# Four-layer kernel: explicit per-engine sequences in place of priorities, two weight pieces moved from the ACT queue to the sync queue, bulk weights on the sync queue

## The chip, the cores and the metric

The kernel runs on one core of one Trainium2 chip. The metric is device microseconds (us) of one execution, the median of several runs. The engines are PE (matrix multiply; PEld is its weight load), DVE (vector), ACT (scalar, with the exponential and the logarithm), POOL (GpSimd) and SP (sync, which here only issues DMAs). Each engine executes its own instruction stream strictly in order and waits on semaphores; a DMA queue of an engine is fed by instructions of that same stream, so an issue that waits holds everything behind it on that engine.

## What is computed

Four layers follow each other on one tensor x of 2048 tokens by 448 features, all in bf16: attention (A), gated MLP (B), attention, gated MLP, each on a layer-normalized x and added back to x. Layers 0 and 2 share the attention weights, layers 1 and 3 the MLP weights.

```python
def _A_ref(x, wqkv, wo):                    # 16 heads of 28, window of 8 tokens, step 2
    qkv = (x @ wqkv).reshape(B, S, 3, H, Dh) ...
    idx = pos[:, None] - (jnp.arange(8) * 2)[None, :]
    logits = jnp.einsum("bhsd,bhswd->bhsw", q, k[idx]) * Dh ** -0.5
    attn = softmax(where(idx >= 0, logits, -1e9))
    return einsum("bhsw,bhswd->bhsd", attn, v[idx]) ... @ wo
def _B_ref(x, w_gate, w_up, w_down):        # F = 1792
    return ((x @ w_gate) * (x @ w_up)) @ w_down

x = x + _A_ref(_layernorm(x), wqkv, wo); x = x + _B_ref(_layernorm(x), w_gate, w_up, w_down)
x = x + _A_ref(_layernorm(x), wqkv, wo); x = x + _B_ref(_layernorm(x), w_gate, w_up, w_down)
```

## The kernel before

**Tiling.** Tokens are cut into chunks of 256 or 512 per layer (`ACH`, `BCH`); a chunk of layer l is called A0j, B1j, A2j or B3j, and `SEQ` gives the order in which chunks are planned (A00 A01 B10 A02 B11 ...), so that layers overlap. A matmul uses 64 of the 128 rows of the array, and two of them run side by side on the two halves; "a pair" below means such two. The main tiles are these.

- Layer norm (`ln_chunk`, L772 to L809): DVE takes statistics (`bn`, `mv`), ACT a logarithm and an exponential (`lnv`, `rstd`), DVE writes `xn_sb`. For layer 0 PE transposes it (L803, "Tps" below) and DVE or ACT copies the result to `xnTa` (L809, "T"). Later layers transpose by DMA on SP (L796).
- Query and key (`qk_chunk`): PE multiplies `xnTa` by `WQK`; one of ACT and DVE copies the bank pair to `qk` (L895, "QK(layer, chunk, part)"). Four rows of some parts are written to a DRAM tensor `vt` by small DMAs on SP (L904) and read back transposed (L915), as a part of the values.
- Value (`v_group`, L987), scores (`attn_front`: PE L1007, "S"; ACT exponential L1014; DVE mask L1024), attention times value (`attn_back`: PE L1044, "AV"; copies L1055; normalization L1069 to L1082), output projection (`y_blocks`, "Y", x updated at L1099).
- MLP (`b_chunk`): a unit is 14 matmuls of `xnTb` by `WGU` (gate and up on the two halves), then ACT copies the gate (L1135), DVE multiplies by up into `hT` (L1138), and PE multiplies `hT` by `WD` ("D").

L534 is the helper `pair` from which nearly all large matmuls are issued. L537 is its strip form: a score or AV burst of 64 small matmuls can be woven with large matmuls cut into four strips of 32 columns each (`WEAVE`).

**PSUM.** Eight banks; most users take a pair, and a bank is free again when its last reader has run.

**The order of the work.** `Sched` holds every operation with its dependencies and an estimated time. `schedule` runs the estimates as a simulation while the program is built; in before, whenever an engine is free it picks the ready operation of the lowest priority number (`prio` plus the tables `PR`, `XP`, `JP`, `HEAD_P`, `ATT_P`), with limits on banks (`A_CAP`, `B_CAP`). What comes out is a fixed order for each engine, and `emit` writes it with semaphore waits. At run time there is no choice: the program is the order.

**The head.** x and the weights come by DMA in pieces: x block 0 ("x0"), block 1 ("x0b"), blocks 2 and 3 ("x0h"), then blocks 4 to 7, 8 to 11 and 12 to 15 ("x1", "x2", "x3"). The query/key weights come in four pieces into a staging area in `hT` (`load_stage`, "stg0" to "stg3"), and eight copies (L709, "wqk(piece, half)") on ACT, DVE and POOL spread them into `WQK`; L717 ("wqp") adds the rows for `vt` later and has to wait until the query/key matmuls of chunk A01 are done, since they read the same tile. PE meanwhile runs 25 filler pairs on zeros (`WARM + FILL`, L700). POOL also builds masks (`MT`, `MK`) and a tile of ones (`ones32`, key `c_ones`), which a DMA on SP writes to `vt` ("vones", L624).

**The bulk weights** are `wo_g` (output projection), `WGU` (gate and up, two halves each: wg0, wu0, wg1, wu1) and `WD` (wd0 to wd3). In before they wait for x block 8; wg goes on SP and wu on ACT at once, `wo_g` waits for wu1 to land, wd0 for `wo_g`, and each next wd for the one before.

## Time and profile before

| | us |
|---|---|
| median of 3 runs | 391.18 |
| all three | 390.90, 391.18, 392.06 |
| the profiled execution | 392.05 |
| its span, first to last instruction | 390.3 |

The granted PE clock is 1.000 over the whole span. The table by stretches of the span (us; PE, DVE and ACT are busy times) shows where PE is not busy:

| stretch | PE | DVE | ACT | DMA GB/s |
|---|---|---|---|---|
| 0 to 9 | 7.74 | 5.17 | 4.85 | 248 |
| 9 to 16 | 6.47 | 6.95 | 4.34 | 287 |
| 16 to 46 | 28.07 | 23.14 | 26.76 | 156 |
| 46 to 75 | 26.39 | 24.47 | 19.32 | 53 |
| 75 to 390 | 312.85 | 216.18 | 145.52 | 38 |

In the last row PE is busy for 99.3% of the time. What is not busy before 75 us is 1.26 + 0.53 + 1.93 + 2.61 = 6.33 us. In views by line, a row names line, engine, operation, output<-input and count, then busy time and mean nanoseconds, then the idle time of the engine in front and what ended it.

### The profile page before, as it was taken

To read this page: it belongs to the slowest core of one execution; us is meant where nothing else is said; L and a number is where in the kernel's file an instruction comes from. 1 tells how busy PE (TensorE), PEld (TensorE's weight loads), DVE (VectorE), ACT (ScalarE), POOL (GpSimd) and SP (SyncE) were. 2 spreads that over 40 slices of the span, in tenths; PEclk is the share of its full clock that TensorE was granted. 3 is DMA by queue.
4 is the path that set the end of the run, shared out by engine and by line. 5 is a ranking of instruction groups with operands and counts; after the bars stand their busy time and mean duration, and the time that the engine had idled before them with its cause. 6 is when DMAs were issued, how large, how long until landed. Compare 5 with 4: busy or idle time off the path is not lost.

```text
span 390.3 us, 14405 instructions
## 1 busy us (share of the span) xinstructions
PE 381.5 (98%) x6394; PEld 213.8 (55%) x6394; DVE 275.9 (71%) x606; ACT 200.8 (51%) x386; POOL 8.3 (2%) x38
## 2 busy tenths in 40 slices
PE   8999989999999999999999999999999999999997
PEld 3555468554555544544456678545445544544584
DVE  6976789899649798496459965287676875467452
ACT  4797886664506676053544645055642542344150
POOL 7010000000000000000000000000000000000000
PEclk9999999999999999999999999999999999999999
DMA  7973532404302413221150204403230212100201
GB/s 258 263 210 92 131 41 56 58 11 83 41 2 53 61 21 50 49 29 29 22 55 15 41 13 33 82 26 52 37 64 29 40 34 50 50 2 2 51 23 47
DMA packets 54753, 22.50 MB, mean 58 GB/s; under 512 B 44884, under 2 KB 54692, under 8 KB 54692
## 3 DMA queue, kind: packets, MB, share of 16 engines
q1 hardware_dynamic: 53188, 19.24, 25.8%
q10 hardware_dynamic: 1504, 2.35, 2.2%
q8 instruction: 50, 0.82, 0.9%
q14 instruction: 11, 0.09, 0.1%
HBM read 8.54 MB, written 2.71 MB: 29 GB/s over the span
## 4 chain that ended last, share of the span: by engine, by line
PE 93%; ACT 4%; DVE 2%; issue 1%; ACTq 0%; DVEq 0%
PE ps L534 83%; PE ps L1007 3%; PE ps L1044 2%; PE ps L700 2%; PE ps L537 2%; PE ps L1150 1%; ACT qk L895 1%; ACT xnTa L809 1%; ACT E_sb L1014 1%; ACT R_sb L1070 0%; ACT g_sb L1135 0%; DVE oT L1082 0%; ACT O_sb L1055 0%; DVE v_sb L987 0%; DVE R_sb L1069 0%
## 5 line engine op out<-in xcount | busy, mean ns | idle before, releaser
L534 PE MATMUL ps<-xnTb,WGU 64*128 64x512 bf16 (+1 forms) x1942 | 176.8, 333 | 0.8 <-issue 0.8
L534 PEld LDWEIGHTS ps<-xnTb,WGU 64*128 64x128 bf16 x1942 | 94.2, 94 | 72.1 <-issue 1.5
L1135 ACT ACTIVATE g_sb<-ps 128x512 bf16<-128x512 f32 (+1 forms) x140 | 71.1, 511 | 92.9 <-PE ps L534 87.7
L1138 DVE TENSOR_TENSOR hT<-g_sb,ps 128x512 bf16<-128x512 bf16 (+1 forms) x140 | 79.6, 575 | 35.9 <-ACT g_sb L1135 34.0
L534 PE MATMUL ps<-WD,hT 64*128 64x448 bf16 x824 | 81.8, 349 | 0.0
L1099 DVE TENSOR_TENSOR x_sb<-x_sb,ps 128x448 bf16<-128x448 bf16 x62 | 35.9, 616 | 40.9 <-PE ps L534 40.8
L534 PEld LDWEIGHTS ps<-WD,hT 64*128 64x128 bf16 x824 | 39.6, 94 | 36.0
L534 PE MATMUL ps<-xnTa,WQK 64*128 64x512 bf16 (+1 forms) x488 | 51.6, 352 | 0.3 <-ACT xnTa L809 0.2
L1014 ACT ACTIVATE E_sb<-ps 128x1024 bf16<-128x1024 f32 (+1 forms) x36 | 33.7, 981 | 20.9 <-PE ps L1007 20.6
L772 DVE BATCH_NORM_STATS2 st<-x_sb 128x6 f32<-128x448 bf16 x64 | 37.4, 610 | 1.6 <-DMA x_sb<-in_A_x_dram 1.6
L793 DVE TENSOR_SCALAR xn_sb<-x_sb,mv,rstd 128x512 bf16<-128x512 bf16 (+1 forms) x64 | 34.1, 570 | 0.9 <-ACT rstd L777 0.8
L534 PEld LDWEIGHTS ps<-xnTa,WQK 64*128 64x128 bf16 x488 | 22.9, 94 | 20.5 <-ACT xnTa L809 1.1
L895 ACT ACTIVATE qk<-ps 128x1024 bf16<-128x1024 f32 (+1 forms) x30 | 26.9, 923 | 10.5 <-PE ps L534 10.3
L534 PE MATMUL ps<-wo_g,oT 64*128 64x448 bf16 x252 | 29.3, 349 | 0.1
L1024 DVE TENSOR_TENSOR E_sb<-E_sb,MK 128x1024 bf16<-128x1024 bf16 (+2 forms) x40 | 23.7, 608 | 7.2 <-ACT E_sb L1014 7.0
L1082 DVE TENSOR_TENSOR oT<-O_sb,R_sb 128x480 bf16<-128x480 f32 (+3 forms) x36 | 21.6, 627 | 5.2 <-ACT R_sb L1071 4.7
L1055 ACT ACTIVATE O_sb<-ps 128x512 f32<-128x512 f32 (+3 forms) x22 | 11.5, 547 | 26.4 <-PE ps L1044 26.3
L1070 ACT ACTIVATE R_sb<-R_sb 128x480 f32<-128x480 f32 (+1 forms) x34 | 20.0, 601 | 8.6 <-DVE R_sb L1069 8.5
L1069 DVE STREAM_SHUFFLE R_sb<-O_sb 128x480 f32<-128x480 f32 (+1 forms) x34 | 22.3, 696 | 0.0
L534 PE MATMUL ps<-WV,xnTa 64*128 64x336 bf16 (+3 forms) x244 | 21.1, 304 | 0.2
L1071 ACT ACTIVATE R_sb<-R_sb 128x480 f32<-128x480 f32 (+1 forms) x34 | 19.6, 601 | 0.4
L534 PEld LDWEIGHTS ps<-wo_g,oT 64*128 64x128 bf16 x252 | 12.5, 94 | 11.8 <-DVE oT L1082 1.1
(59 smaller groups left out, 190.7 us busy)
## 6 DMA issues: line engine op xcount, KB each, us to landing
out_dram<-x_sb SPq DMA_DIRECT2D x15, 112.0 KB, 1.7
WGU<-in_B_w_up_dram ACTq DMA_DIRECT2D x2, 784.0 KB, 11.5
WGU<-in_B_w_gate_dram SPq DMA_DIRECT2D x2, 784.0 KB, 13.5
x_sb<-in_A_x_dram SPq DMA_DIRECT2D x3, 448.0 KB, 7.1
WD<-in_B_w_down_dram SPq DMA_DIRECT2D x2, 448.0 KB, 3.8
hT<-in_A_wqkv_dram ACTq DMA_DIRECT2D x3, 224.0 KB, 3.5
WD<-in_B_w_down_dram SPq DMA_DIRECT2D x2, 336.0 KB, 3.9
vt<-qk SPq DMA_DIRECT2D x42, 16.0 KB
```

The lines of the kernel that those rows point to most:

```text
L534: return lambda E: E.matmul(out(), lhs(), rhs(), start=start, stop=stop)
L772: sc.add("dve", one(lambda E, B=B: E.bn_stats(st6[:, B, :], x_sb[:, B, :]), ("bn", li, B)), 525.0, deps=[("x", li - 1, B)] + ([("xn", li - ...
L793: sc.add("dve", one(lambda E, B=B, dst=dst, src=src: E.tensor_scalar(dst, src, mv[:, B, 0:1], rstd[:, B:B + 1], ALU.subtract, ALU.mult), ( ...
L895: return E.activation(dst, src, ACT.Copy) if hasattr(E, "activation") else E.tensor_copy(dst, src)
L1014: return E.activation(E_sb[:, slot, 2 * hp:2 * hp + 2, 0:w], ps[:, b0:b0 + 2, 0:w], ACT.Exp, scale=SCALE)
L1024: return E.tensor_tensor(e, e, m, ALU.mult)
L1069: sc.add("dve", one(lambda E: E.stream_shuffle(R_sb[:, rs, 0:w], O_sb[:, os_, 0:w], [DH] * 32), ("Rs", li, qb)), dve_est(w) + 100.0, deps= ...
L1070: sc.add("act", one(lambda E: E.activation(R_sb[:, rs, 0:w], R_sb[:, rs, 0:w], ACT.Ln), ("Rl", li, qb)), act_est(w, False), deps=[("Rs", l ...
L1082: return E.tensor_tensor(oT[:, :, a % HALF:a % HALF + z - a], O[:, :, a - tok:z - tok], R_sb[:, rs, 0:w].rearrange("p (h n) -> p h n", h=4 ...
L1099: sc.add("dve", one(lambda E: E.tensor_tensor(x_sb[:, B, :], x_sb[:, B, :], ps[:, bk[w], 0:D], ALU.add), ("x", li, B)), dve_est(D), deps=[ ...
L1135: sc.add("act", one(lambda E, gs=gs, bk=bk: E.activation(g_sb[:, gs, 0:nt], ps[:, bk[0], 0:nt], ACT.Copy), ("G", li, j, fc)), act_est(nt), ...
L1138: sc.add("dve", one(lambda E, gs=gs, bk=bk, fc=fc: E.tensor_tensor(hT[:, fc, hs, 0:nt], g_sb[:, gs, 0:nt], ps[:, bk[1], 0:nt], ALU.mult), ...
```

## The change

Every priority table is taken out. The new table `ORD` lists the operations of each engine by number, in the order in which they are to stand ("a+b" on PE is a woven couple), and `schedule` takes the next number of an engine when its operands and banks are ready in the simulation. Operations that may run on two or three engines are thereby also assigned to one. The filler falls from 25 to 22 pairs. Two of the four query/key weight pieces (stg0, stg2) stay on the ACT queue and now stand ahead of ACT's table load; the others (stg1, stg3) are on SP behind x0 and x0b. All bulk weights are on SP: `wo_g` first, then wg0, wu0, wg1, wu1, then `WD` with the same waits on each other as before, wd0 now waiting for wu1. The remaining edits are constants of the build-time simulation (`LINE_T`, `VONES_L`, `BL`, landing times); they produce no instruction.

```diff
-FILL = 16
+FILL = 13
+ORD = {
+    "pe": "44 45 46 47 48 49 50 51 52 53 54 55 56 57 58 104 59 60 61 107 62 63 64 65 193 195 197 194 199 196 122 ...",
+    "act": "2 3 14 97 98 101 102 67 105 108 113 114 201 119 123 204 120 202 126 207 208 129 132 236 ...",
+    "dve": "15 16 17 95 96 99 100 103 68 106 69 111 109 112 110 115 117 121 116 118 133 124 135 203 ...",
+    "pool": "22 21 23 18 27 38 39 19 20 31 40 66 70 71 34 73 72 35 24 41 28 29 25 32 36 26 30 42 33 77 75 76 81 37 43 80",
+    "sp": "0 1 4 5 6 7 8 9 10 11 12 13 82 83 84 85 86 87 88 89 90 91 360 575 355 291 293 503 574 501 572 504 500 92 ...",
+}
...
-                op = best
+                op = item[0]
...
-    load_stage("act", 0, 3400.0)
-    load_stage("sp", 1, 5950.0)
-    load_stage("act", 2, 4350.0)
-    load_x(0, 2, 4, "d_x0h", 6550.0)
-    load_stage("act", 3, 6150.0)
+    load_stage("act", 0, 3600.0)
+    load_stage("act", 2, 4200.0)
+    load_stage("sp", 1, 5300.0)
+    load_stage("sp", 3, 5800.0)
+    load_x(0, 2, 4, "d_x0h", 6400.0)
...
+    for j in range(4):
+        dst = wo_g[32 * j:32 * j + DH, :, :]
+        src = A_wo.rearrange("(c j e) d -> j e c d", c=4, j=4, e=DH)[j]
+        bulk("sp", dst, src, ("wo", j), f"d_wo{j}", BULK_AFTER, WOL)
+    lats = iter(BL)
...
-                last = bulk(("sp", "act")[w], WGU[64 * w:64 * w + 64, a:z, f0:f1], W_[64 * a:64 * z, f0:f1].rearrange("(k p) f -> p k f", p=64), (("wg", "wu")[w], n, m), f"d_w{'gu'[w]}{n}{m}", BULK_AFTER, BL[0])
-    for j in range(4):
-        dst = wo_g[32 * j:32 * j + DH, :, :]
-        src = A_wo.rearrange("(c j e) d -> j e c d", c=4, j=4, e=DH)[j]
-        prev = bulk("sp", dst, src, ("wo", j), f"d_wo{j}", [last], BL[1])
+                prev = bulk("sp", WGU[64 * w:64 * w + 64, a:z, f0:f1], W_[64 * a:64 * z, f0:f1].rearrange("(k p) f -> p k f", p=64), (("wg", "wu")[w], n, m), f"d_w{'gu'[w]}{n}{m}", BULK_AFTER, next(lats))
```

Operation numbers that the prediction speaks of: 43 is `c_ones`, 82 vones, 83 to 86 `wo_g`, 87 to 90 wg0, wu0, wg1, wu1, 91 to 94 wd0 to wd3, 66 to 73 the copies wqk(0,0), wqk(0,1) ... wqk(3,1), 75 to 81 wqp, 14 ACT's table load.

In the order that results, compared with before: on POOL `c_ones` stands behind four wqp copies, which wait for the query/key matmuls of A01 (before, it stood ahead of all masks); wqk stands five times on POOL, twice on DVE and once on ACT (before 2, 2 and 4). Of the 36 copies L895, 16 are on DVE and 20 on ACT (before 6 and 30), of the 16 copies L809, 11 on ACT and 5 on DVE (before 7 and 9). 13 of the 18 AV bursts are woven (before 16): in layer 0 those of groups 1 to 4 no longer are, and that of group 5 now is.

## The prediction

> **What bounds the kernel now.** I read the page's busy times first, then who PE waited for, then the timeline of the head and of the stretches where PE stood still, and last the rows by shape for prices.

> ```profile
> PE 381.5 (98%) x6394; PEld 213.8 (55%) x6394; DVE 275.9 (71%) x606; ACT 200.8 (51%) x386; POOL 8.3 (2%) x38
> q8 instruction: 50, 0.82, 0.9%
> ```

> PE is busy for 381.5 of 390.3 us, and a warm pair of 512 columns starts every 0.216 us almost throughout, so the matmuls themselves are the floor, and an order can win little beyond the idle time: 1.26 + 0.53 + 1.93 + 2.61 us before 75 us and 2.15 after. The second row is the queue that brings PE's instructions: 50 packets for 12,928 instructions (two for each of 6394 matmuls, and 140 waits), so one packet holds about 256 of them ("a line" below).

> ```profile
> PE ps L1044 <- issue: 1.7, 2, 1.0
> PE ps L534 <- issue: 0.8, 1, 0.8
> PE ps L1007 <- ACT E_sb L1014: 0.6, 1, 0.6
> PE ps L803 <- ACT qk L895: 0.5, 2, 0.3
> ```

> ```profile
> 50.92 0.22 PE L1044 MATMUL ps<-E_sb,v_sb 64*32 64x64 bf16 x7 [0.96 <-issue]
> 54.98 1.27 PE L534 MATMUL ps<-xnTb,WGU 64*128 64x256 bf16 x20 [0.77 <-issue]
> 72.54 0.24 PE L1044 MATMUL ps<-E_sb,v_sb 64*32 64x64 bf16 x12 [0.77 <-issue]
> ```

> The first fence is the view of waits of PE, the second its timeline. The largest waits are put down to nothing ("issue"). Counting PE's instructions, they stand at 1985, 2240 and 3009, which is 7.75, 8.75 and 11.75 lines: each at the same place of a line. The packets of the instruction queue before them start at 48.17, 52.37 and 70.05, and PE goes on 2.75, 2.61 and 2.49 later. From start to start these waits are 1.12, 0.93 and 0.94 longer than normal, 3.0 in all: PE ran out of instructions, in lines that hold only 2.69, 2.80 and 4.06 us of matmuls because score and AV bursts fill them. The other waits are on ACT.

> ```profile
> 0.81 1.28 ACT L621 ACT_TABLE_LOAD   x1 [0.81 <-PEq L1266]
> 0.85 1.35 ACTq L624 DMA_DIRECT2D hT<-in_A_wqkv_dram  x3
> 7.24 1.04 ACT L709 ACTIVATE WQK<-hT 128x448 bf16<-128x448 bf16 x2 [1.21 <-DMA hT<-in_A_wqkv_dram]
> 8.19 0.58 ACT L809 ACTIVATE xnTa<-ps 128x512 bf16<-128x512 bf16 x1
> 8.82 2.03 PE L534 MATMUL ps<-xnTa,WQK 64*128 64x256 bf16 x34
> 10.34 0.71 ACTq L726 DMA_DIRECT2D WGU<-in_B_w_up_dram  x1
> 23.50 1.09 POOL L717 COPY WQK<-hT 128x64 bf16<-128x64 bf16 x6 [13.57 <-PE ps L803]
> ```

> In the timeline of the head, ACT copies two weight pieces at 7.24, then a transpose at 8.19, and only then the first query/key matmul starts.

> **The change part by part.** The sum is made on the profiled execution, 392.05, and carried to the median by its distance, 0.87.

> *DMAs ahead of the table load.* The ACT queue already issued its first piece at 0.85, while the load ran from 0.81 to 2.09. There is 0.05 at most to win, and a load that ends some 0.9 later (two issues of 0.45) is done before ACT's first statistics at 4.43: 0.

> *Start of the query/key matmuls.* The pieces land at 3.83, 4.76, 7.22 (stg1) and 7.42 (stg3). In the new order stg3 follows stg1 on SP and passes x0h; the same bytes precede it (x0, x0b, four pieces), so I keep 7.42. What follows is two POOL copies of 0.556, to about 8.55, in place of 8.82: -0.3. Bounds: -0.65 if all operands are early and only the three filler pairs (0.216 each) count; +0.25 if stg3 lands with x0h, at 7.89. x0h itself, one issue (0.43) later, stays behind the same total of bytes.

> *9 to 16 us.* PE waits 0.35, 0.35 and 0.3 (at 13.40, 13.89, 14.45), as four transposes in a row need copies. The new order spreads them between query/key matmuls, and ACT no longer issues wu: the chain of waits has 0.30 and 0.10 of these issues. Against it, three of the copies L809 move from DVE (0.42) to ACT (0.60). Walking ACT's new list with these durations gives the first scores about 0.3 earlier relative to the head: -0.3, between -1.0 (all three waits) and +0.9 (ACT paces every transpose).

> *16 to 46 us.* ACT is busy 26.76 of 30.

> ```profile
> L895 ACT ACTIVATE qk<-ps 128x1024 bf16<-128x1024 f32 x23 | 23.1, 1023 | 9.1 <-PE ps L534 8.9
> L895 DVE CAST qk<-ps 128x1024 bf16<-128x1024 f32 x5 | 6.1, 1224 | 3.2 <-PE ps L534 3.2
> ```

> Four of the large copies in this stretch go to DVE at 1.224; with the transposes and O_sb copies that go the other way ACT falls to about 24 and DVE rises from 23.14 to about 26.6. The waits from start to start here are 0.35, 0.3, 0.65, 0.23, 0.3, 0.45 and 0.78. The last two (41.15, 42.06) come because score group S(0,6) follows S(0,4) after only two transposes, before the exponentials (2 x 1.02) free its banks; the new order puts 20 matmuls of 512 columns (2.2 us) between them, which removes up to 1.23. I take -0.9; bounds -1.7 (0.5 more, of the others) and +0.8 (four copies bind on DVE, 0.2 each).

> *Lines of instructions.* With the cadences of the trace (N/2.4 + 2.6 ns per pair, 9 ns per burst matmul) the lines between 23 and 75 us hold 4.75, 4.81, 6.42, 3.42, 4.79, 4.70, 4.93, 5.12, 5.52 and 4.41 us in the new order. A line is enough if it is longer than the delay of its packet behind the start of the line plus 2.6. These delays are 1.0 to 2.8 in this stretch, and 1.44, 3.86 and 1.61 while the bulk weights fly. Averaged over these rows the new lines lack 0.2, 0.25, 0, 1.2, 0.16, 0.2, 0.12, 0.06, 0 and 0.3, about 2.2 together, against 3.0 now: -0.8. Bounds: -2.0 (only the 3.42 line stalls, 1.0) and +3.2 (below).
> [...]

> *Weaving.* Three fewer AV bursts are woven. A woven burst takes 0.94 (the chain of waits, 101.46 to 102.40) with two pairs inside; 73 burst matmuls without strips take 0.84 at 70.93, so 64 take 0.74, and two pairs 0.43: 0.23 more each. The burst at the 9 ns cadence gives 0.07. +0.5; bounds 0.2 and 0.7.

> *Bulk on SP, late.* vones waits for `c_ones`, and in the new POOL list that stands behind four wqp copies, which wait for A01's matmuls: 23.5 + 4 x 0.23 + 0.32 (mask) + 0.20, about 24.5 instead of 8.86. `wo_g`, wg, wu and wd0 stand behind vones: issues of 0.91, 2.31 and four of about 1.4 end near 33.4. Before, 3.2 MB took from 10.40 to 26.63, so the last piece lands near 25.4 + 16.2 = 41.6. Work that hides it: wo_g is first used at 35.70 (lands near 29), WGU at 53.95. A weight that came later would cost its lateness outright. Next on SP are wd0 and the small writes. The writes of chunk A03 hold SP until its last copy on DVE, by cadence 2.5 before the first MLP matmul (54). From there: 6 writes of 0.345, wd1, 9 writes, wd2, four L915 transposes (2.2 + 3 x 1.25), a write, wd3; each wd lands 3.2 to 4.5 after issue (median 3.8). So wd3 lands 15.5 to 17.9 after that copy, and the first D matmul, which needs it, stands 16.4 after it. +0.4; bounds 0 and 1.5. Before, wd3 had landed at 45.35.
> Moving wu from ACT to SP costs no bandwidth I can see: both queues shared the same interval.

> *After 75 us* PE idles 2.15 of 315, the tail included; 0, +-0.6. Constants: 0.

> Sum: -0.3 - 0.3 - 0.9 - 0.8 + 0.5 + 0.4 = -1.4, so 390.65 for a profiled execution and **389.8** at the median.

> **The rivals.**
> *The late bulk starves PE of instructions* (slower). The bulk now flies from 25 to 42, across lines of 4.81, 6.42 and 3.42; before, it flew across lines of 6.2, 7.2 and 5.0 that hid it. If every such packet is as late as the one at 20.45 (3.86 behind its line's start, ready at 6.6 by the waits' mean), they lack 1.8, 0.2 and 3.2, with 1.0 for the rest 6.2 against 3.0: +3.2 in place of -0.8, **393.8**. It decides from a delay of about 3 us. For it: that row. Against it: 1.44 and 1.61 beside it. [...]
> *DVE takes ACT's place.* At 26.6 of 30 DVE is where ACT was, and the 16 to 46 term is 0 to +0.8: 390.7 to 391.5. For it: DVE's copy costs 0.2 more. Against: the S(0,6) wait is of order, not of load.
> *SP comes last.* Its chain has almost no slack at the first D and at AV group 5 (0.5 by the same count): +1.5 instead of +0.4, 390.9. Its cover of ten us in before is gone. Against: only upper durations give it.
> *The new order is no better, only other* (the change doesn't do what it says): waits move, weaving is lost, 391 to 391.7.

> **How the numbers follow.** Forecast, faster by over 0.3% (below 390.0; 0.3% is about what a measurement here can tell): 0.40, and 0.06 that several lower bounds meet, near 387.5. Late bulk 0.22, all slower. DVE 0.14, SP 0.10, no better 0.08: of these 0.20 fall within 390.0 to 392.35 and 0.12 go above it, where two of them meet. So faster 0.46, same 0.20, slower 0.34. The range runs from 387 (the lower bounds of half the terms) to 394 (the first rival); the forecast's own is 388.3 to 390.8.

> **What would show it.** The first query/key matmul near 8.5. vones issued near 24.5 and the last WGU piece landed near 42; if it stands near 9, my reading of POOL's order is wrong. PE's "issue" waits summing to about 2, mostly at the short line near 44; sums over 4 and lying between 28 and 46 mean the first rival. No wait of S(0,6) on the exponential. A wait of the first `WD` matmul on a DMA means SP. The prediction is wrong if PE's idle time before 75 us is not below 5.5 us.

## The result and the profile after

The changed kernel has a median of 394.5 us over 20 runs (390.6 to 398.5); the kernel before, on the same chip, 391.0 over 20 (390.0 to 393.9). The ratio is 1.0067, 95% interval 1.0045 to 1.0090: slower, where 389.8 and faster were forecast. The profiled execution took 397.53, span 395.8, so it is one of its longer runs, as the profiled one of before (392.05) was.

Runs of one kernel differ by the granted clock: "runs at full clock" below are those whose mean clock over the span is 0.999 or more, and a ratio leaves out runs far above a kernel's fastest, while a median holds all. The changed kernel has 4 of 20 (390.6 to 392.5 us); twelve lie at 0.995 or 0.996 (393.1 to 395.5), four at 0.991 (395.6 to 398.5). The kernel before, in all the runs of it made for this study after that, has 116 of 118.

The page of the changed kernel, its busy times and two rows of its 40 slices:

```profile
PE 384.9 (97%) x6352; PEld 213.2 (54%) x6352; DVE 287.6 (73%) x616; ACT 188.1 (48%) x374; POOL 10.1 (3%) x40
...
PE   8999699899999999999999999999999999999996
...
PEclk9999799999999999999999999999999999999999
```

PE does the same matmuls (42 fewer, the filler and the woven strips) in 3.4 us more, and the fifth slice (39.6 to 49.5 us) has both less work and a lower clock. PE's view of waits names the place:

```profile
PE ps L491 <- issue: 4.0, 2, 3.5
PE ps L491 <- DVE mv L732: 1.3, 1, 1.3
```

L491 is the helper `pair`, L534 in before. Windows of 2 us (busy time and count of PE, PEld, DVE, ACT, POOL, then clock, DMA share, GB/s) and PE's timeline show what happens:

```profile
40.00:42.00 2.00, 1.70 (x44) 0.78 (x36) 1.55 (x3) 1.63 (x2) 0.00 (x0) 1.00 1.07 211
42.00:44.00 2.00, 0.00 (x0) 0.00 (x0) 2.00 (x4) 0.31 (x1) 0.00 (x0) 1.00 1.07 203
44.00:46.00 2.00, 0.78 (x4) 0.30 (x5) 0.52 (x3) 0.00 (x0) 0.00 (x0) 0.58 0.45 87
46.00:48.00 2.00, 2.00 (x72) 0.97 (x70) 0.00 (x0) 0.12 (x1) 0.00 (x0) 0.50 0.27 53
```

```profile
40.23 1.47 PE L491 MATMUL ps<-xnTa,WQK 64*128 64x512 bf16 x12
45.22 1.89 PE L491 MATMUL ps<-xnTa,WQK 64*128 64x512 bf16 x8 [3.52 <-issue]
47.04 0.80 PE L964 MATMUL ps<-qk 28*64 28x64 bf16 x64
47.77 3.56 PE L491 MATMUL ps<-xnTa,WQK 64*128 64x512 bf16 x16
```

From 41.7 to 45.2 PE does nothing and waits for nothing that the profile shows; all DMA engines are busy (share 1.07) at 203 to 211 GB/s. The packet of PE's instruction queue starts at 42.22 and PE goes on 3.0 later. Then the clock is at half: twelve pairs of 512 columns up to 50.7 start every 0.427 us instead of 0.216, and a score burst between them takes 0.80 instead of 0.64, which together costs 2.7 us more. What SP does explains the DMA load:

```profile
23.82 0.91 SPq L581 DMA_DIRECT2D vt<-ones  x1
24.85 2.54 SPq L683 DMA_DIRECT2D wo_g<-in_A_wo_dram  x4
27.43 0.73 SPq L683 DMA_DIRECT2D WGU<-in_B_w_gate_dram  x1
...
29.55 1.15 SPq L683 DMA_DIRECT2D WGU<-in_B_w_up_dram  x1
46.29 0.40 SPq L683 DMA_DIRECT2D WD<-in_B_w_down_dram  x1
...
71.16 0.41 SPq L683 DMA_DIRECT2D WD<-in_B_w_down_dram  x1
```

vones goes out at 23.82 (8.86 in before), and wd0, which waits for wu1, at 46.29: the bulk flies from 25 to 46. Its four gate and up pieces land 3.2 to 3.9 us apart, one after the other. The rates while these pieces fly (40 slices of the window, then its packets and mean) are, before from 10.4 to 26.6 us:

```profile
GB/s 383 369 321 304 246 215 224 351 261 217 204 204 195 190 199 243 235 204 217 204 243 336 363 372 425 341 327 345 358 376 310 270 217 199 102 58 94 63 22 2
DMA packets 3450, 3.97 MB, mean 245 GB/s; under 512 B 1152, under 2 KB 3445, under 8 KB 3445
```

and after from 27.4 to 46.3:

```profile
GB/s 230 197 156 95 95 163 322 258 193 221 193 182 193 239 224 201 193 209 186 190 193 243 228 197 205 197 190 193 197 228 231 221 209 178 190 193 133 49 34 0
DMA packets 2207, 3.52 MB, mean 186 GB/s; under 512 B 106, under 2 KB 2205, under 8 KB 2205
```

Before, a phase at 200 GB/s is followed by one at about 330 to 425; after, nearly all is at 200. The 1.3 us put down to `mv` is the first D matmul at 76.16, 1.45 late from start to start: wd3, issued at 71.16, lands at 73.7 to 75.9, so it is WD that came last.

### The profile page after: what moved, and what is told of

It is laid out like the page before. It is cut to its first block, busy times and chain, and to the rows that moved or that the text cites. A ratio compares the mean times of both kernels' runs of the same rounds, so it can differ in the third digit from the quotient of the medians.

```text
span 395.8 us, 14241 instructions
## 1 busy us (share of the span) xinstructions
PE 384.9 (97%) x6352; PEld 213.2 (54%) x6352; DVE 287.6 (73%) x616; ACT 188.1 (48%) x374; POOL 10.1 (3%) x40
## 4 chain that ended last, share of the span: by engine, by line
PE 92%; ACT 3%; DVE 2%; issue 1%; DMA 1%
PE ps L491 83%; PE ps L964 2%; PE ps L657 2%; PE ps L1001 2%; PE ps L1107 1%; PE ps L494 1%; DMA xnTb<-xn_sb 1%; ACT qk L852 1%; ACT xnTa L767 1%; ACT O_sb L1012 1%; PE ps L761 0%; DVE R_sb L1026 0%; DVE st L730 0%; DVE x_sb L1056 0%; DVE qk L852 0%
## 5 line engine op out<-in xcount | busy, mean ns | idle before, releaser
L491 PE MATMUL ps<-xnTb,WGU 64*128 64x512 bf16 (+1 forms) x1946 | 177.7, 333 | 0.1
L491 PEld LDWEIGHTS ps<-xnTb,WGU 64*128 64x128 bf16 x1946 | 94.3, 94 | 72.7 <-DVE hT L1095 1.0
L1092 ACT ACTIVATE g_sb<-ps 128x512 bf16<-128x512 f32 (+1 forms) x140 | 69.5, 510 | 104.4 <-PE ps L491 85.3
L1095 DVE TENSOR_TENSOR hT<-g_sb,ps 128x512 bf16<-128x512 bf16 (+1 forms) x140 | 77.5, 573 | 36.5 <-ACT g_sb L1092 36.0
L491 PE MATMUL ps<-WD,hT 64*128 64x448 bf16 x820 | 84.7, 349 | 1.4 <-DVE mv L732 1.3
L491 PE MATMUL ps<-xnTa,WQK 64*128 64x512 bf16 (+1 forms) x500 | 54.9, 364 | 4.1 <-issue 4.0
L491 PEld LDWEIGHTS ps<-WD,hT 64*128 64x128 bf16 x820 | 39.2, 94 | 36.3 <-issue 1.5
L491 PEld LDWEIGHTS ps<-xnTa,WQK 64*128 64x128 bf16 x500 | 24.2, 96 | 27.6 <-issue 6.9
L751 DVE TENSOR_SCALAR xn_sb<-x_sb,mv,rstd 128x512 bf16<-128x512 bf16 (+1 forms) x64 | 35.3, 566 | 3.8 <-ACT rstd L735 3.7
L981 DVE TENSOR_TENSOR E_sb<-E_sb,MK 128x1024 bf16<-128x1024 bf16 (+2 forms) x40 | 23.6, 609 | 10.1 <-ACT E_sb L971 10.0
L491 PE MATMUL ps<-wo_g,oT 64*128 64x448 bf16 x244 | 27.9, 350 | 0.1
L852 ACT ACTIVATE qk<-ps 128x1024 bf16<-128x1024 f32 (+1 forms) x20 | 17.3, 874 | 16.8 <-PE ps L491 16.6
L852 DVE CAST qk<-ps 128x1024 bf16<-128x1024 f32 (+1 forms) x16 | 18.7, 1186 | 7.6 <-PE ps L491 7.4
L491 PE MATMUL ps<-WV,xnTa 64*128 64x336 bf16 (+3 forms) x252 | 23.0, 304 | 0.0
L491 PEld LDWEIGHTS ps<-wo_g,oT 64*128 64x128 bf16 x244 | 11.5, 94 | 11.4 <-PE ps L491 0.5
```

Source lines behind the costliest of these rows:

```text
L491: return lambda E: E.matmul(out(), lhs(), rhs(), start=start, stop=stop)
L751: sc.add("dve", one(lambda E, B=B, dst=dst, src=src: E.tensor_scalar(dst, src, mv[:, B, 0:1], rstd[:, B:B + 1], ALU.subtract, ALU.mult), ( ...
L852: return E.activation(dst, src, ACT.Copy) if hasattr(E, "activation") else E.tensor_copy(dst, src)
L981: return E.tensor_tensor(e, e, m, ALU.mult)
L1092: sc.add("act", one(lambda E, gs=gs, bk=bk: E.activation(g_sb[:, gs, 0:nt], ps[:, bk[0], 0:nt], ACT.Copy), ("G", li, j, fc)), act_est(nt), ...
L1095: sc.add("dve", one(lambda E, gs=gs, bk=bk, fc=fc: E.tensor_tensor(hT[:, fc, hs, 0:nt], g_sb[:, gs, 0:nt], ps[:, bk[1], 0:nt], ALU.mult), ...
```

## The experiments

They ask in turn: is it that the bulk is late (1, 2), that it is on one queue (3 to 7), the order of work or the head (8, 9), what stands in the queue (10, 12, 16), when the bulk starts (11, 13 to 15), and the queue alone with the bulk late (17). In the edits of the kernel before, its order was written out as a list and its banks kept, so that one thing changes at a time; in those of the changed kernel order and banks are its own but for the numbers shown. "Line n" is the packet that the instruction queue starts as its n-th after 9 us.

**e1: the ones early.** On POOL `c_ones` (43) stands ahead of the masks again.

```diff
-    "pool": "... 20 31 40 66 ... 81 37 43 80",
+    "pool": "... 20 31 43 40 66 ... 81 37 80",
```

> The changed kernel with one POOL instruction moved: the memset of the ones (c_ones) goes from behind the four wqp copies (23.6 us) to the position before c_mk0 work of the head, so that the vones DMA and with it the whole bulk can start at about 9 to 10 us. Theory 'late bulk' (the bulk transfers of 25 to 46 us keep PE's instruction line of 42.2 us back, and the clock drops after the 3.5 us of idle time): wu1 landed by about 27 us, no PE stall over 1 us between 28 and 50 us, granted clock of 16 to 46 and 46 to 75 us back at 0.99 or more, no 1.45 us wait at the first WD matmul; time 388.5 to 390.8, 0.990 of the changed kernel. Rival 'one queue' (all bulk on SP is too slow wherever it starts): the stall comes back somewhere between 12 and 40 us, 393 to 396. Rival 'another order of work' (DVE and ACT): the stalls of 45 us stay and the time is 393.5 to 395.

394.1 us (10 runs, one at full clock), ratio 1.0073 [1.0049, 1.0097]. The bulk is early (wo_g issued at 9.94, last WGU piece landed at 31.4), and PE stops in another place. Its windows:

```profile
24.00:26.00 2.00, 0.33 (x44) 0.33 (x43) 1.50 (x6) 0.58 (x3) 0.00 (x0) 1.00 1.05 191
26.00:28.00 2.00, 2.00 (x45) 1.17 (x43) 0.53 (x1) 1.58 (x2) 0.00 (x0) 0.71 1.09 219
28.00:30.00 2.00, 2.00 (x14) 0.93 (x12) 0.53 (x2) 1.57 (x4) 0.00 (x0) 0.50 1.02 188
```

PE stands from 23.98 to 25.67 (line 2 starts at 22.90), then runs at half clock. The WD wait is gone (0.3). So the theory that lateness alone does it fell: as much is lost with the bulk early.

**e2: the ones late, but behind the bulk.** `c_ones` stays late, vones moves behind wu1 on SP.

```diff
-    "sp": "... 13 82 83 84 85 86 87 88 89 90 91 360 ...",
+    "sp": "... 13 83 84 85 86 87 88 89 90 82 91 360 ...",
```

> The changed kernel with the vones DMA moved on SP behind wu1 (before wd0); c_ones stays late at 23.6 us, so vones goes out at about 24 us but the wo, gate and up pieces at 9 to 13 us. Theory 'late bulk': as with the memset moved, 388.5 to 390.8, because only the DMA that waited stood ahead of the bulk. If instead c_ones itself or vones matters: 393 to 395.

394.5 (12 runs, one at full clock), 1.0087 [1.0058, 1.0116]: as e1, with stalls of 1.31 at 24.4 and 1.83 at 32.7. It is not vones itself.

**e3 and e4: the kernel before with all bulk on SP**, early and, in e4, with `c_ones` behind four wqp copies.

```diff
-last = bulk(("sp", "act")[w], WGU...
+last = bulk("sp", WGU...
-prev = bulk("sp", dst, src, ("wo", j), f"d_wo{j}", [last], BL[1])
+bulk("sp", dst, src, ("wo", j), f"d_wo{j}", BULK_AFTER, BL[1])
```

> The kernel before, order of every engine and every bank kept, with the bulk as in the change: wo first, then the four gate and up pieces, all on SP, wd0 behind wu1; c_ones early as before. Theory 'late bulk': the queue is not the cause, 390 to 392 (before: 391). Rival 'one queue': 393 or more, with a PE stall at a line end between 12 and 40 us.

> As the one before it, and c_ones moved on POOL behind four of the six wqp copies, as in the change (about 24 us). Theory 'late bulk': bulk from 25 to 46 us as in the changed kernel, a PE stall of 2 to 4 us at a line end between 30 and 50 us and a granted clock below 0.97 behind it, 393.5 to 397. Rival 'one queue': like the one before it, within 0.5 us. Rival 'another order of work': 391, since order and banks are those of before.

e3: 396.3 (6 runs, none at full clock), 1.0125 [1.0093, 1.0157]. e4: 404.2 (6 runs, none at full clock), 1.0328 [1.0294, 1.0362]. The waits of PE in e3:

```profile
PE ps L509 <- issue: 5.3, 2, 4.5
```

The order of before, which loses 3.0 us to late lines, loses 4.5 us more in one place (line 3 starts at 30.39, PE goes on at 33.34) once up stands on SP's queue: the new order of work is not needed for the loss. The four pieces take 19.1 us from the first issue to the last landing (14.06 to 33.13), 16.2 in before. In e4 two lines are late (stalls of 3.56 and 2.66; the profile names an ACT logarithm for the second, but it stands at the first instruction of a line and 2.87 behind that line's packet), and an `xnTb` transpose comes late on SP (3.36 at 65.5).

**e5: two queues, but each with the same half of the partitions.** SP issues gate 0 and up 0, ACT gate 1 and up 1.

```diff
-last = bulk(("sp", "act")[w], WGU...
+last = bulk(("sp", "act")[n], WGU...
```

> The kernel before with its two queues kept, but sorted otherwise: SP issues gate 0 and up 0, ACT gate 1 and up 1, so that both queues write partitions 0 to 63 first and 64 to 127 after that. All else as before. Theory 'half of the partitions' (a transfer to 64 partitions runs at about 205 GB/s, 3.9 us for a piece of 784 KB, and while such pieces alone run, PE's next instruction line comes 5 to 7 us late): WGU landed at 29 us or later, about 200 to 220 GB/s all through, a PE stall of 2 us or more at a line end before 35 us, 392.5 to 396. Theory 'one queue' (the number of queues sets the rate): as before, WGU landed by 26.6, 300 GB/s or more in 18 to 24 us, no such stall, 390.5 to 391.8.

391.4 (10 runs, all at full clock), 1.0028 [1.0007, 1.0049]; no stall at a line end before 50 us, last piece landed at 27.25. Its rates from 10 to 27 us:

```profile
GB/s 375 372 319 290 296 253 354 223 198 202 198 190 190 202 202 202 202 202 232 299 346 367 375 422 236 219 198 198 194 202 198 211 198 190 198 177 129 117 42 21
```

About 200 while two gate pieces run together (14 to 18 us), 350 to 420 while a gate and an up piece do, about 200 again for two up pieces. So here the half of the partitions sets the rate, and two queues do not. It did not set the stalls: I had expected them to go together.

**e6: the changed kernel on two queues.** e1 with gate ahead of `wo_g` on SP and up on ACT.

```diff
-    "act": "... 113 114 201 119 123 ...",   "sp": "... 13 82 83 84 85 86 87 88 89 90 91 ..."
+    "act": "... 113 114 201 88 119 90 123 ...",   "sp": "... 13 82 87 89 83 84 85 86 91 ..."
```

> The changed kernel with the memset of the ones early, the two gate pieces ahead of wo on SP, and the two up pieces back on ACT behind the first qk copy, so that gate (partitions 0 to 63) and up (64 to 127) run together from about 10 us, as before the change. Both theories: WGU landed by 27 us, the stalls of 1.9 us at 25.7 and of 0.7 at 32.9 gone, granted clock 1.0 in most runs, 389 to 391. If the time stays at 393 to 395, the other order of work is the cause, and neither theory holds.

5 of 12 runs are at full clock (390.0 to 391.4), the others take 393.2 to 399.4; ratio 1.0021 [0.9990, 1.0051]. The profile is of a run at full clock (span 388.3) and its largest late line costs 0.68.

**e7: one queue, finer.** e1 with each gate and up piece in three, in turn.

```diff
-KP = ((0, 7),)
+KP = ((0, 2), (2, 4), (4, 7))
```

> The changed kernel with the memset early and all bulk on SP as in the change, but each gate and up piece cut into three (k 0-2, 2-4, 4-7), gate and up in turn. Theory 'half of the partitions': pieces of 224 to 336 KB of both halves overlap more in the queue, rate between 205 and 350 GB/s, WGU landed by 29 us, stalls at 25.7 and 32.9 smaller, 390 to 393. Theory 'one queue': 205 GB/s and the stalls as with the memset moved, 393 to 395.

394.1 (4 runs, one at full clock), 1.0079 [1.0056, 1.0102]; 212 to 232 GB/s throughout, a stall of 2.85 at 30.96 (line 3 starts at 28.03). Cutting into three did not help while all of it stood in the queue at once.

**e8: the head alone** on the kernel before.

```diff
-    load_stage("act", 3, 6150.0)
+    load_stage("sp", 3, 5800.0)
-    "act": "14 2 4 6 ...",   "sp": "0 1 3 5 ..."
+    "act": "2 4 14 ...",   "sp": "0 1 3 6 5 ..."
```

> The kernel before with the head of the change alone: on ACT the two weight pieces 0 and 2 ahead of the table load, piece 3 on SP behind piece 1 (ahead of the x blocks 1 to 3). Order and banks else as before. My step in the prediction: -0.3 us at most (first QK matmul 8.55 instead of 8.82); from the trace of the changed kernel (9.00) rather 0 to +0.2. Time 390.6 to 391.6; first QK matmul between 8.5 and 9.1.

390.2 (10 runs, all at full clock), 0.9989 [0.9969, 1.0008]; first query/key matmul at 8.58 in its profile. The time can't be told from no change.

**e9: the changed kernel with the bulk of before.** e6, with `wo_g` behind wu1 and wd0 behind `wo_g`.

```diff
-bulk("sp", dst, src, ("wo", j), f"d_wo{j}", BULK_AFTER, WOL)
+bulk("sp", dst, src, ("wo", j), f"d_wo{j}", [("wu", 1, 0)], WOL)
-..., f"d_wd{n}", [prev], WDL)
+..., f"d_wd{n}", [prev if n else ("wo", 3)], WDL)
```

> The changed kernel (its head, its order on every engine, its banks) with the bulk as it was before the change: ones early, gate on SP and up on ACT, wo behind the landing of the last up piece, wd0 behind the last wo piece. Theory 'bulk' (what the bulk does to PE's instruction lines is all that the change loses, the rest gains): profile span 388 to 389.5 like that with two queues, but with granted clock 1.0 in nearly all runs, 389 to 390.6, ratio 0.995 to 1. Rival 'order' (the new order itself is what lets the clock drop in more than half of the runs): again runs of 393 to 399 at clocks of 0.996 and below, median over 392.

390.6 (6 runs, four at full clock: 389.9 to 391.1; the others 395.0 and 397.4), 1.0008 [0.9963, 1.0054]. No late line in the profile (span 388.2), a WD wait of 1.52 at 68.7. With the bulk of before, the new order loses nothing and gains nothing that these six runs can measure; but it falls more often into the lower clock than before does.

**e10: one piece at a time on the one queue.** e1, each gate and up piece behind the landing of the one ahead.

```diff
-..., f"d_w{'gu'[w]}{n}{m}", BULK_AFTER, next(lats))
+..., f"d_w{'gu'[w]}{n}{m}", [prev] if (n, w) != (0, 0) else BULK_AFTER, next(lats))
```

> The changed kernel with the memset early and all bulk on SP as in the change, but each gate or up piece waits for the landing of the one ahead of it, so that never more than one piece is in the queue. Theory 'depth of the queue' (PE's instruction line waits behind what stands in the one queue: 6 to 10 us with four pieces in it): the line comes at most 4 us late (28 packets of 0.14 us per DMA engine), no PE stall over 1 us before 50 us, WGU landed near 38 to 40 us, 389.5 to 391.5, clock 1.0 in most runs. Theory 'one queue, whatever stands in it': lines 6 us late as with the memset moved, stalls of 1 to 3 us between 24 and 45 us, 393 to 395.

391.3 (6 runs, all at full clock, 390.5 to 392.4), 1.0012 [0.9981, 1.0042]. SP's issues:

```profile
11.78 1.43 SPq L689 DMA_DIRECT2D WGU<-in_B_w_gate_dram  x1
19.18 0.60 SPq L689 DMA_DIRECT2D WGU<-in_B_w_up_dram  x1
26.12 0.60 SPq L689 DMA_DIRECT2D WGU<-in_B_w_gate_dram  x1
32.79 0.60 SPq L689 DMA_DIRECT2D WGU<-in_B_w_up_dram  x1
```

The pieces' first DMA engines are done at 18.59, 25.37, 32.33 and 38.56; lines 2 to 5 start at 18.10, 24.81, 31.77 and 38.11, each 0.45 to 0.56 before: the four lines that came due during a piece started when that piece was nearly through. The worst costs 1.31 us, where a stall of at most 1 was expected. This is the changed kernel's one queue, and the loss is nearly gone.

**e11: WD early.** e9 with wd1 to wd3 right behind wd0 on SP.

```diff
-    "sp": "... 86 91 360 575 ... 500 92 499 ... 502 93 369 ... 571 94 569 ...",
+    "sp": "... 86 91 92 93 94 360 575 ... 500 499 ... 502 369 ... 571 569 ...",
```

> The changed kernel with the bulk as before the change (ones early, gate on SP and up on ACT, wo behind the last up piece), and beyond that the four WD pieces issued in a row ahead of the first vt transfers on SP, instead of the last one at 65 us. Expected: the wait of 1.5 us of the first WD matmul near 69 us gone, WD landed by 46 us, span of an undisturbed run 1 to 1.7 us below that with the bulk of before (388.2), so 388.3 to 389.5 at clock 1.0; a third of the runs may still fall to clocks of 0.996 with 393 to 397, since nothing here changes what the instruction lines meet up to 28 us. If WD was not what the first WD matmul waited for, the time stays at 390 to 391.

The first D matmul no longer waits (0.30), and one run took 388.6; but 11 of 12 were below full clock: median 395.2, ratio 1.0037 [1.0001, 1.0073]. Up to 28 us this program is that of e9. The profile here is of a run at 0.991; its windows, and then those of e9:

```profile
16.00:18.00 2.00, 1.58 (x12) 0.48 (x13) 2.00 (x9) 1.92 (x6) 0.00 (x0) 1.00 1.05 211
18.00:20.00 2.00, 0.00 (x0) 0.00 (x0) 2.00 (x8) 0.20 (x1) 0.00 (x0) 1.00 1.05 338
20.00:22.00 2.00, 0.20 (x2) 0.12 (x3) 0.59 (x3) 0.00 (x0) 0.00 (x0) 0.60 1.05 348
```

```profile
16.00:18.00 2.00, 2.00 (x22) 0.89 (x20) 2.00 (x9) 1.63 (x4) 0.00 (x0) 1.00 1.06 278
18.00:20.00 2.00, 2.00 (x28) 0.98 (x26) 1.70 (x7) 2.00 (x4) 0.00 (x0) 1.00 1.07 378
20.00:22.00 2.00, 1.88 (x44) 0.99 (x40) 2.00 (x5) 1.85 (x6) 0.31 (x2) 1.00 1.06 306
```

In e9 the first query/key matmul ran at 7.84 and line 1 started at 11.65; in e11 at 8.98, and line 1 did not start before 19.22, two us after the first gate piece (issued at 10.17) had landed. PE stood 4.38 us. The heads of these two profiles lie a microsecond apart; my theory was that whether line 1 asks ahead of the bulk or behind it hangs on that, and e13 and e14 test it.

**e12: two pieces under way.** e11 with the second gate and up piece both on SP, each behind the first of its kind.

```diff
+..., f"d_w{'gu'[w]}{n}{m}", [(("wg", "wu")[w], 0, 0)] if n else BULK_AFTER, next(lats))
```

> As the one before it, but the second gate and the second up piece both on SP and each behind the landing of the first of its kind, so that never more than two pieces are under way, of different halves. Theory 'depth of the queue': instruction lines at most 4 us late, none of the runs below clock 0.999, 388.3 to 390 in all of them. If the drops of the clock come from something else (the order, the head), a third of the runs at 0.996 and 393 to 397 as with the bulk of before.

396.3 (6 runs, none at full clock), 1.0112 [1.0073, 1.0150]. The second pair went out at 21.2 and 21.9, line 3 started at 30.53 and PE stood 4.92 us. Two pieces in one queue are enough, and my expectation was wrong: I had taken "of different halves" for what matters.

**e13 and e14: the start of the bulk.** e11, with the gate and up pieces behind the fourth query/key copy (e13) or behind x block 4 and ahead of the first such copy (e14). The up issues on ACT move with them, and in e14 vones goes behind the gate pieces on SP.

```diff
-BULK_AFTER = [("x", -1, 8)]
+BULK_AFTER = [("x", -1, 8), ("QK", 0, 0, 3)]      # e13
+BULK_AFTER = [("x", -1, 4)]                       # e14
```

> The kernel with WD early once more, all as there, but the gate and up pieces wait for the fourth qk copy of the head (about 12 us) instead of the x block alone (about 10 us), so that the bulk always comes after the moment when PE asks for its instruction line 2 (1.2 us after line 1 starts at 9.6 to 10.8). Theory 'a line that asks behind the first bulk piece waits for it' : line 2 comes at 11 to 12.5 us in every run, no stall of 4 us near 18, clock 0.999 or more in nearly all runs, 388.3 to 390, faster than before by 0.3 to 0.5%. If the drops of the clock come from elsewhere: half of the runs at 0.996 or less, 393 to 397, as with WD early.

> The same with the gate moved the other way: gate and up pieces wait for x block 4 only and stand ahead of the ones on SP and ahead of the first qk copy on ACT (issued near 8.5 to 9 us). Theory 'a line that asks behind the first bulk piece waits for it': line 2 comes behind the first pieces in every run, at 15 us or later, a stall of 1 to 5 us near 16 to 22 us, clock 0.996 or less in most runs, 392 to 397. If where the bulk starts does not decide it: the same mix of runs as with WD early.

e13 (pieces issued from 13.1): 10 of 12 runs at full clock, median 391.2, 1.0022 [1.0008, 1.0037]. e14 (from 8.3): 1 of 4, median 393.1, 1.0069 [1.0050, 1.0089]; line 1 at 16.08, a stall of 2.15. Both ran on one chip (e9 and e11 each on another), so on it a later start goes with more runs at full clock; e14 has only four. The theory of the request is less clear: in e13's profile line 1 started at 14.07, behind the issue of the first pieces, where 11 to 12.5 was expected, and no stall followed. That e13 is no faster than before has a cause of its own, seen on ACT:

```profile
13.08 1.38 ACTq L689 DMA_DIRECT2D WGU<-in_B_w_up_dram  x2
14.51 0.20 ACT L741 ACTIVATE rstd<-lnv 128x2 f32<-128x2 f32 x1 [1.51 <-issue]
```

Two issues hold ACT, an `rstd` waits for them, DVE's `xn` for that, and PE 1.2 us for the `xn`.

**e15: the late gate with the issues moved** behind that rstd.

```diff
-    "act": "... 204 88 90 120 202 126 207 208 129 132 ...",
+    "act": "... 204 120 202 126 88 207 208 129 90 132 ...",
```

> The kernel with the late gate again, with the two up transfers on ACT moved behind the next rstd (one behind the fourth x copy, one three V copies later), because in the profile of the late gate they held ACT for 1.38 us at 13.1 and PE waited 1.3 us for the xn that came after. Theory 'instruction line' unchanged: clock 0.999 or more in nearly all runs; the 1.3 us wait gone; 389 to 390.3, faster than before by 0.1 to 0.4%. If the wait at 15.5 only moves: 390.5 to 391.5 as before this edit.

11 of 12 runs at full clock, 390.5, ratio 0.9996 [0.9982, 1.0009]. The wait is gone and WD's too. Of the versions of the changed kernel it has the lowest median, and it is level with the kernel before.

**e16: eight pieces, one at a time.** e10 with `KP = ((0, 4), (4, 7))` and wd2, wd3 a little earlier.

> The changed kernel with the memset early and all bulk on SP, no transfer on ACT, but in eight gate and up pieces of 336 to 448 KB, each behind the landing of the one ahead, and the last two WD pieces issued about 6 us earlier. Theory 'a line waits for the piece that is in the queue' : with pieces half as long lines are at most 3 us late, no PE stall over 0.7 us before 50 us except the known one at 22.3, clock 0.999 or more in all runs, the WD wait of 1.7 us gone; WGU landed near 47 us; 389 to 390.3. If lines wait for something else than the piece in the queue: stalls of 1 us or more at 30 to 46 us as with four chained pieces, 390.5 to 392.

No line comes late: lines 1 to 5 at 11.80, 16.58, 23.50, 27.70 and 31.62, and no stall over 0.7 before 50 us. But the time is 394.9 to 397.7 in five runs, none at full clock (a sixth took 2200 us and is left out), 1.0156 [1.0132, 1.0181]. PE's waits:

```profile
PE ps L497 <- DMA xnTb<-xn_sb: 3.3, 2, 3.0
PE ps L1007 <- DMA v_sb<-vt: 2.7, 1, 2.7
```

SP waits out eight landings up to 49.54, and the transposes behind them come late. The expectation held for the lines, and not for the time (389 to 390.3).

**e17: the changed kernel with up on ACT again, and nothing else undone.**

```diff
-    "act": "... 243 244 219 167 220 567 ...",   "sp": "... 86 87 88 89 90 91 ..."
+    "act": "... 243 244 219 88 167 220 90 567 ...",   "sp": "... 86 87 89 91 ..."
```

> The changed kernel with one part undone: the two up transfers are issued on ACT again (near 27.2 and 28.5 us), all else as in the change, the late memset of the ones included, so that gate and up run together on two queues from about 27.5 us. If the move to one queue alone is what costs, lines come at most 4 us late, WGU lands by 40 us, no PE stall over 2 us, 390 to 392. If the late time costs too (the lines met from 25 to 42 us last 4.8, 5.1 and 7 us and bear only 1.8 to 4 us of lateness, where those of 10 to 24 us last 6 and 7), there is a stall of 1 to 4 us at a line end near 33 to 42 us and the clock drops in many runs, 393 to 396.

395.7 (4 runs, none at full clock), 1.0135 [1.0110, 1.0160]. Its windows:

```profile
34.00:36.00 2.00, 0.00 (x0) 0.00 (x0) 2.00 (x4) 0.81 (x2) 0.00 (x0) 1.00 1.05 242
36.00:38.00 2.00, 0.60 (x4) 0.30 (x5) 0.23 (x1) 0.00 (x0) 0.00 (x0) 0.64 1.07 286
38.00:40.00 2.00, 2.00 (x13) 0.80 (x10) 0.00 (x0) 0.00 (x0) 0.00 (x0) 0.50 1.08 203
```

Line 4 starts at 34.62 (28.09 in e9), PE goes on at 37.40 after 3.74 us and at half clock. The last piece landed at 45.65, 20.2 us after the first issue (25.41), so the second queue brought no speed here: from 28 to 34 us ACT's queue, with both up pieces, moved 1.03 MB and SP's, with the gate pieces and the rest of `wo_g`, 0.25. So late on two queues is no better than late on one.

## Why the prediction was wrong

Some of the late lines of these profiles, taken together (packet start, next matmul of PE, what the gap was over normal, in us):

| run | line starts | PE goes on | later by | stall |
|---|---|---|---|---|
| after, line 4 | 31.68 | 34.74 | 3.06 | 0.62 |
| after, line 5 | 42.22 | 45.22 | 3.00 | 3.68 |
| e1, line 2 | 22.90 | 25.67 | 2.77 | 1.88 |
| e3, line 3 | 30.39 | 33.34 | 2.95 | 4.66 |
| e4, line 5 | 45.23 | 48.10 | 2.87 | 2.66 |
| e7, line 3 | 28.03 | 30.96 | 2.93 | 2.85 |
| e10, line 4 | 31.77 | 34.53 | 2.76 | 1.31 |
| e11, line 1 | 19.22 | 21.80 | 2.58 | 4.38 |
| e17, line 4 | 34.62 | 37.40 | 2.78 | 3.74 |

The others (e2, e4's line 4, e12, e14) lie between 2.58 and 3.07. A packet takes 0.88 to 1.66 us once it starts (all 50 of before; 0.88 to 1.52 in the result), with the bulk in flight or without; what is late is its start. The nearly fixed 2.6 to 3.1 us tie each of these stalls to that packet.

**The direction and its cause.** The first rival, "the late bulk starves PE of instructions", is what happened; that its 393.8 is so near 394.5 is luck, since it priced 6.2 us of late lines and no clock, and the profile has 4.3 and a clock drop. Two more things of it were wrong. It put the cause to the late time alone. The runs show the loss on one queue early (e1, e2, e3) as well as late (after, e4), and late on two queues too (e17). Early on two queues it is there in the profiles of e11 and e14 and not, or only as 0.68 us (e6), in those of e5, e6, e9, e13 and e15. And it took a packet to be at most 3.86 late behind the start of the line ahead; by the same count line 5 of the changed kernel is 8.3 late (42.22 against 33.90).

**The step that failed** is the term on the lines of instructions, -0.8. It averaged the delays of three lines of before, 1.44, 3.86 and 1.61, and took the average for lines that would meet another arrangement of the bulk. The delay that mattered was 8.3, and the late lines cost 3.68 + 0.62 against 3.0, so +1.3. (The ten shortfalls it lists also add to 2.49 and not to 2.2, which makes it -0.5 on its own figures.) Behind it stands the sentence that moving wu from ACT to SP costs no bandwidth, since both queues shared the same interval. Early it does cost some: in before the two queues, with two halves of the partitions, ran together at about 330 to 425 GB/s for part of the time, and with all on SP the pieces took 19.1 us instead of 16.2 (e3). Late, as in the change, they took 18.9 and landed at 46.3 instead of the 41.6 forecast; 2.0 of that is that the first gate piece went out at 27.43, behind the issues of `wo_g`, and not at the 25.4 of the working, and 2.7 is the slower flight. That two queues would have flown faster at that time is not shown: in e17 they took 20.2.

**A term was missing.** Nothing in the sum priced the clock. After 3.5 us without a matmul it fell to half, which cost 2.7 us on top of the stall's 3.68. That is the profiled run, at a mean clock of 0.991; twelve of the 20 runs lie at 0.995 or 0.996, and a profile at that clock (e1) has one step of 3.413 us at half clock where this one has two, so they lost at most about 1.7 us to it, an estimate (half of one step). The four runs at full clock take 390.6 to 392.5; none of them has a profile, so their stalls are not known. For the two profiles (397.53 against 392.05, +5.5) the lines, the clock, the first D matmul and the start of the query/key matmuls add to 1.3 + 2.7 + 1.45 + 0.2 = 5.65, which leaves about -0.2 for the terms whose forecast was -0.7 together (9 to 16, 16 to 46, weaving).

**The late end of SP** (+0.4, bounds 0 and 1.5) lay at its upper bound: the first D matmul waited 1.45. It is not the late wd0: e9, where that goes out at 28.88, waits 1.52 all the same. It is the place of wd1 to wd3 behind the vt transfers, as the working had it; with them moved ahead (e11) 0.30 is left.

**vones** went out at 23.82, forecast about 24.5, for the reason given (POOL's order); the terms written down for it add to 24.9.

**The start of the query/key matmuls** (-0.3): 9.00 in the profile of the result. The working had stg3 land at 7.42 and two POOL copies end the wait; stg3 landed at 6.82, and PE went from the last filler straight into the query/key matmuls. Their start goes with the moment at which the clock rises to full under the filler (in before the filler pairs start 0.427 us apart up to 5.07 and 0.216 from 5.41 on), and that moment differs from run to run. In the 14 profiles of the changed head it lies between 4.00 (e14) and 7.18 (e13), and the query/key matmuls start between 7.63 and 9.20 in the same order of runs but for one pair 0.01 apart, about half a microsecond later for each microsecond. At a like rise, 5.38 in e7 and 5.31 in before, they start at 8.31 and 8.82: 0.5 earlier, near the bound of -0.65 for operands that are early. The 9.00 goes with a rise at 6.78.

**16 to 46 us** (-0.9): the waits on S(0,6) are gone but for 0.35 at half clock, as forecast; the three late lines of before at 50.9, 55.0 and 72.5 are gone too. No run prices these terms, or the 0.5 of weaving, apart. Their sum is bounded by e9 and e15, where the rest of the change stays: 1.0008 [0.9963, 1.0054] and 0.9996 [0.9982, 1.0009]. In e15, without the WD wait, the forecast gain of 1.8 us (the sum without its bulk term) would be 0.9954, outside the interval: most of it is not there, or the two issues on ACT that e15 keeps take it back. Which term falls short was not tried. DVE did not take ACT's place: it is busy 25.5 of 30 us, and PE's longest wait on a copy of it is 0.5.

**After 75 us**: 4.4 us without a matmul up to 395.8 against 2.5 before, of which 1.45 is WD.

Of the signs named in advance, the issue waits lying between 28 and 46 and summing to 4.0 pointed to the first rival, the D matmul on a DMA to SP, and PE's idle time before 75 us, 6.5, was above the 5.5 named as the bound.

What stays open is first why a line starts only when nearly a whole piece is through (e10). Second, why the program of e9 and e11, the same up to 28 us, falls below full clock in 2 of 6 and in 11 of 12 runs (on two chips), and that of before in 2 of 118, although e9 and before both start line 1 near 11.7 in their profiles. Whether line 1 asks ahead of the bulk does not sort the profiles: counted as in the prediction, from when PE begins the line ahead (an estimate: no trace shows when a line is asked for), it asked 0.57 us after the first bulk issue in e11 and 1.08 after it in e14 and came 8.5 and 6.7 later, but in e5 it asked 0.73 after it and came 1.7 later. e13 and e15 show that a later start of the bulk goes with full clock, and not by which step.

## What to carry to other kernels

Before moving weights between queues, look at which transfers run side by side, not only at their bytes: two pieces to different halves of the partitions gave 350 to 420 GB/s here where both queues moved (e5), one after the other about 200 (the changed kernel), and behind several queued pieces PE's next line came 6 to 8 us after PE had begun the line ahead (6.1 and 6.3 in e1, 8.3 in the changed kernel). What lost least here was one large piece at a time (e10; with eight smaller ones in e16 the waits moved to SP's later transfers), or two queues with a start some 3 us later (e15). And a stall of PE of about 3 us is to be priced twice, once as it is and once as the half clock behind it (3.68 and 2.7 us in the profile of the result).
